# Agent attention and a two-level mixture of experts: first layers of 33 tiles over 128 and 19 rows, and one pool of eight PSUM banks

## Chip, cores and metric

The kernel runs on one core of a Trainium2 chip. The metric is the device time of one execution in microseconds, the median of three runs. One further execution was profiled; all durations and waits below come from it.

## The reference

Four batches of 10048 query rows go through an agent attention and then, each row alone, through the one expert of 16 that a two-level router picks for it. Cut to what matters:

```python
# attention, per batch: 49 agents stand between queries and keys
agent_v = sm(agents, k) @ v                 # 49 x 128
x = sm(q, agents) @ agent_v                 # 10048 x 128

# router: best of 4 groups, then best of 4 experts in it
g_idx = argmax(x @ w_group);  e_idx = argmax(x @ w_expert[g_idx])
h = relu(x @ w1[g_idx, e_idx])              # 128 -> 1024
out = g_weight * e_weight * (h @ w2[g_idx, e_idx])   # 1024 -> 128
```

## The kernel before

**Numbers in two halves.** Matrix products with fp16 operands take a value as a high and a low fp16 half. A row of `x` is 49 exponentials times `agent_v`, so the kernel never forms `x`: it folds `agent_v` into the expert's first layer. For each batch, `weights_of` makes a first-layer weight of 49 rows x 1024 columns, doubled to 98 rows, its high half in `ws[:, 0:F]` and its low half in `ws[:, F:2F]`. `query_turn` turns the 49 exponentials' high and low halves into columns: a tile `et` has 98 rows (high, low) and 512 columns, one for each query row.

**Units and tiles.** Most rows of batches one, two and three are computed as if all went to the batch's most frequent expert (`natural`); 20 tiles of 512 rows a batch. A tile has eight units of 128 hidden columns. `first` does a unit's first layer: two products over 98 rows, `et` with the high weights and `et` with the low weights, summed in one PSUM bank `ph`. ScalarE writes relu as fp16 (`hh`), VectorE what is left of it (`hl`). `second` does the unit's second layer: 12 products of 128 columns into the bank `po`, which sums the whole tile. In `run`, `second` of a unit comes eight units after its `first` (`LAG`). `rows_out` scales the tile and stores it.

**What stands between units.** `lanes` holds the other work, the attention of the next batch (`agents_of`, `queries_of`), its router, its weights and the sorting of the rows of the last batch; after each unit, `advance` issues as much of it as the tile's place asks. Each engine takes its instructions in the order of the program. Batch four has no tiles of its own: its rows are gathered by expert and computed in the last part, between the last seven tiles of batch three (`BESIDE`).

**PSUM.** There are eight banks. `ps2` has two, for `po` (and for some tiles while the first attention runs alone); `psa` has six, for `ph` and for the tiles `at` of all other products.

**Loads and stores** are issued by SyncE in the program's order: a copy that waits holds up those behind it.

Of the kernel before, what the change touches and what calls it, by code (L numbers as in the profile page):

```python
# [81 lines left out]
LAG = 8  # L82
WAIT = 0.011
# [74 lines left out]
def build(ctx, tc, qT, kT, v, agT, wr, w1, w2, cpk, out):  # L158
# [13 lines left out]
    ps2 = ctx.enter_context(tc.tile_pool(name="ps2", bufs=2, space=PSUM))  # L172
    psa = ctx.enter_context(tc.tile_pool(name="psa", bufs=6, space=PSUM))
# [5 lines left out]
    def bank(b=1):  # L179

        if alone[0] and b == 0:
            turns[0] += 1
            k = turns[0] % 8
            if k in (1, 4):
                return ps2.tile([P, TQ, C], F32, name="po").rearrange("p a c -> p (a c)")
        return psa.tile([P, 512], F32, name="at", tag="at")
# [41 lines left out]
    ohd = [dram.tile([P, NE, NTP], F16, name=f"ohd{i}") for i in range(B)]  # L228
    wall = dram.tile([NE, P, 2 * F], I32, name="wall")
# [170 lines left out]
    def front(b, early, order, later):  # L400
# [34 lines left out]
        for x in order:  # L435
# [23 lines left out]
            elif o in "sZ":  # L459
                xh, xl = hold["x", f"h{c}" if o == "s" else "q"]  # L460
                y = c if o == "s" else len(chunks)
                ps = psa.tile([P, TS], F32, name="ph", tag="at") if y % 5 < 3 else ps2.tile([P, TQ, C], F32, name="po").rearrange("p a c -> p (a c)")
# [186 lines left out]
    def query_turn(b, ci, x, early):  # L649
        t0, t1 = chunks[ci]  # L650
        for h0 in range(t0, t1, TQ):
# [4 lines left out]
            et = (mo.tile([2 * NA, TS], F16, name="ett", bufs=4) if b == LB else etp.tile([2 * NA, TS], F16, name="et"))[:, 0:(h1 - h0) * P]  # L656
            if b == 0 and h0 // TQ % 4 == 1 and not early:
                vec.tensor_copy(out=et, in_=ptr[0:2 * NA, 0:(h1 - h0) * P])
            else:
                act.activation(et, ptr[0:2 * NA, 0:(h1 - h0) * P], AF.Copy)  # L660
# [5 lines left out]
    def logits_of(b, ci):  # L666
# [8 lines left out]
        for t in range(t0, t1):  # L675
            o = pl[:, (t - t0) * NL:(t - t0 + 1) * NL]
            for h in range(2):
                pe.matmul(o, st["et", t // TQ][:, t % TQ * P:(t % TQ + 1) * P], st["rh"][:, h], start=(h == 0), stop=(h == 1))
# [215 lines left out]
    def weights_of(b, to=None, low=None):  # L894
# [7 lines left out]
        for h in range(2):  # L902
# [5 lines left out]
            yield  # L908
        wv = ws[:, 2 * F:].rearrange("p (k h c) -> p k h c", k=FB, h=2)
# [32 lines left out]
    def first(x, k):  # L942

        w = x["n"]
        ps = psa.tile([P, TS], F32, name="ph", tag="at")
        et = x["et"]
        r = x["per"]
        for j in range(r):
            f = (k * r + j) * P
            for h in range(2):  # L950
                pe.matmul(ps[:, j * w * P:(j + 1) * w * P], x["wb"][0:2 * NA, h * F + f:h * F + f + P], et, start=(h == 0), stop=(h == 1))
        n = r * w * P
        hh, hl = [mo.tile([P, TS], F16, name=name, bufs=LAG + 2) for name in ("hh", "hl")]
# [4 lines left out]
    def second(x, k, hh, hl):  # L958

        if k == 0:  # L960
            x["po"] = ps2.tile([P, TQ, C], F32, name="po")
# [471 lines left out]
```

## Time and profile before

| | |
|---|---|
| median of three runs | 929.74 us |
| the three runs | 926.89, 929.74, 929.83 us |
| the profiled execution | 927.01 us |
| its span, first to last instruction | 925.2 us |
| TensorE busy | 884.6 us, 96% of the span |
| VectorE busy | 686.1 us, 74% |
| ScalarE busy | 601.1 us, 65% |
| GpSimd busy | 507.8 us, 55% |
| granted TensorE clock, mean | 0.994 of full |

Busy times are sums over the span, whose stages have different limits. Products on TensorE overlap their neighbours, so a product's own duration is longer than the distance to the next one; distances between starts say what a product costs.

### The profile page before, as it was taken

The page shows a single profiled execution, that of the slowest core. Times are in us where ns is not written, and L with a number is a line of the kernel's source. Part 1 is how long each engine was busy: PE and PEld are TensorE (multiplying, and loading weights), DVE is VectorE, ACT ScalarE, POOL GpSimd, SP SyncE. Part 2 cuts the span into 40 slices and gives each one's busy share as a digit, 9 for nine tenths or more (in the row PEclk, how much of TensorE's full clock was granted, in tenths as well). Part 3 has the DMA queues.
Part 4 walks back from the last instruction along what each step waited for, and adds up shares of the span by engine and source line. Part 5 has one row for each costly group of instructions (what it writes and reads, how often), then busy time and mean ns, then how long its engine had stood idle before and what let it go on. Part 6 is the DMA issues. An engine that isn't in the chain of part 4 may idle for free.

```text
span 925.2 us, 30602 instructions
## 1 busy us (share of the span) xinstructions
PE 884.6 (96%) x12815; PEld 703.9 (76%) x12815; DVE 686.1 (74%) x1340; ACT 601.1 (65%) x1094; POOL 507.8 (55%) x799
## 2 busy tenths in 40 slices
PE   7889999999999999999999999999999999998996
PEld 6667877787868878787777788767777777776785
DVE  7799889866798765689674667999766666664663
ACT  5486686787668768867773987565555555554552
POOL 2242475364027447415731863135778888888883
PEclk9999999999999999999999999999999999999998
DMA  9682355640168462017853301262353343433331
GB/s 343 226 287 92 91 162 157 195 149 17 39 225 292 128 200 79 25 39 251 295 172 97 112 21 39 110 218 70 118 185 128 126 145 113 133 121 118 119 100 40
DMA packets 61925, 129.03 MB, mean 139 GB/s; under 512 B 7063, under 2 KB 38889, under 8 KB 58321
## 3 DMA queue, kind: packets, MB, share of 16 engines
q1 hardware_dynamic: 56592, 119.75, 38.7%
q0 software_dynamic: 5184, 7.23, 2.9%
q8 instruction: 102, 1.67, 0.8%
q14 instruction: 47, 0.38, 0.1%
HBM read 93.83 MB, written 33.29 MB: 137 GB/s over the span
## 4 chain that ended last, share of the span: by engine, by line
PE 58%; DVE 18%; POOL 4%; ACT 3%; DMA 2%; issue 2%; SPq 0%; POOLq 0%; DVEq 0%; ACTq 0%
PE po L142 29%; PE ph L142 19%; PE at L142 11%; DVE hl L142 8%; POOL out L1243 1%; DVE oh L142 1%; ACT hh L142 1%; POOL gap L1222 1%; DMA er<-erow,gidx 1%; POOL er L1206 1%; DMA xf<-kT 1%; DVE rx L142 1%; DVE oa L142 1%; DMA w2f<-w 1%; DVE oo L142 0%
## 5 line engine op out<-in xcount | busy, mean ns | idle before, releaser
L142 DVE SCALAR_TENSOR_TENSOR hl<-ph,hh 128x512 f16<-128x512 f32 (+1 forms) x642 | 430.2, 679 | 175.7 <-ACT hh L142 174.9
L142 PEld LDWEIGHTS <-hh 128*128 128x128 f16 x5088 | 415.1, 97 | 146.7 <-issue 1.3
L142 ACT ACTIVATE hh<-ph 128x512 f16<-128x512 f32 (+1 forms) x642 | 373.3, 595 | 184.6 <-PE ph L142 180.7
L142 PE MATMUL po<-wbuf,hh 128*128 128x128 f16 x4640 | 451.6, 219 | 1.1 <-DVE wbuf L142 1.1
L142 PE MATMUL po<-wbuf,hl 128*128 128x128 f16 x2320 | 417.8, 219 | 0.0
L142 PE MATMUL ph<-et,wbuf 98*128 98x512 f16 (+1 forms) x960 | 282.1, 376 | 7.5 <-DVE hl L142 5.9
L261 POOL TENSOR_TENSOR xl<-xf,xh 128x256 f16<-128x256 f32 x280 | 178.5, 671 | 177.6 <-ACT xh L142 175.8
L142 PEld LDWEIGHTS <-hl 128*128 128x128 f16 x2544 | 247.7, 97 | 2.2 <-issue 1.3
L142 ACT ACTIVATE xh<-xf 128x1024 f16<-128x1024 f32 x78 | 81.7, 1047 | 42.8 <-PE at L142 24.4
L142 PEld LDWEIGHTS <-wbuf 98*128 98x128 f16 x1184 | 90.0, 99 | 20.6 <-issue 17.9
L988 POOL TENSOR_TENSOR oo<-oo,cw 128x256 f32<-128x256 f32 (+1 forms) x62 | 42.0, 699 | 101.6 <-ACT oo L142 91.8
L1206 POOL DMA_INDIRECT er<-erow,gidx x81 | 83.2, 1027 | 19.1 <-issue 13.8
L1243 POOL DMA_INDIRECT out<-oo,sidx x81 | 80.8, 998 | 19.1 <-issue 11.7
L142 PE MATMUL ph<-ets,wbuf 98*128 98x512 f16 (+1 forms) x224 | 64.2, 372 | 0.0
L646 POOL TENSOR_TENSOR rows<-ef,rows 128x147 f16<-128x147 f32 (+1 forms) x108 | 42.6, 424 | 39.4 <-ACT rows L142 39.4
L1222 POOL MEMSET gap<- 128x320 f16 x162 | 62.5, 386 | 0.1
L142 PEld LDWEIGHTS <-xh 128*128 128x128 f16 x1264 | 56.1, 97 | 4.9 <-issue 3.4
L142 PEld LDWEIGHTS <-xl 128*128 128x128 f16 x632 | 50.4, 96 | 3.0 <-POOL xl L261 1.9
L142 PE MATMUL at<-agh,xl 128*128 128x49 f16 x545 | 51.0, 185 | 1.4 <-POOL xl L261 1.4
L142 PE MATMUL at<-agh,xh 128*128 128x49 f16 x545 | 51.4, 185 | 1.0 <-DVE hl L142 1.0
L142 PE MATMUL at<-agl,xh 128*128 128x49 f16 x545 | 51.0, 185 | 0.0
L142 PE MATMUL at<-vf,S 128*49 128x129 f32 (+1 forms) x632 | 43.9, 278 | 2.6 <-ACT S L142 2.5
(291 smaller groups left out, 895.2 us busy)
## 6 DMA issues: line engine op xcount, KB each, us to landing
xf<-qT SPq DMA_DIRECT2D x38, 512.0 KB, 3.7
vf<-v SPq DMA_DIRECT2D x36, 516.0 KB, 5.0
xf<-kT SPq DMA_DIRECT2D x35, 512.0 KB, 7.0
out<-oo SPq DMA_DIRECT2D x57, 256.0 KB, 3.7
wbuf<-wall SPq DMA_DIRECT2D x14, 1024.0 KB, 4.8
wsg<-wall SPq DMA_DIRECT2D x7, 1024.0 KB, 5.4
erow<-rows SPq DMA_DIRECT2D x3, 1975.0 KB, 8.9
w2f<-w SPq DMA_DIRECT2D x6, 512.0 KB, 4.8
```

Of the source, the lines that this page charges most:

```text
L142: y = f(*a, **k)
L261: eng.tensor_sub(out=xl[:, y], in0=xf[:, y], in1=xh[:, y])
L646: (vec if whole else pool).tensor_sub(out=rows[:, w, NA:2 * NA], in0=ef[:, y], in1=rows[:, w, 0:NA])
L988: pool.tensor_mul(out=o[:, y], in0=o[:, y], in1=state[b]["cw"][:, t + y.start:t + y.stop].broadcast_to([P, y.stop - y.start, C]))
L1206: ins = pool.indirect_dma_start(out=er[:, q], out_offset=None, in_=erow[b][:, :], in_offset=bass.IndirectOffsetOnAxis(ap=place(b, col + q) ...
L1222: tc.keep_in_program_order(pool.memset(gap, 0.0))
L1243: ins = pool.indirect_dma_start(out=out, out_offset=bass.IndirectOffsetOnAxis(ap=place(x["b"], x["col"] + q)[1], axis=0), in_=o[:, q], in_ ...
```

## The change

For tiles of batch two (20) and batch three (13, up to the last seven), the first layer of a unit is cut differently. The product of the low exponentials with the low weights is left out (a term of the size of both halves' rounding). What stays has 98 + 49 = 147 rows: both halves of the exponentials with the high weights, and the high exponentials with the low weights. 128 of them go into one product: rows 98 to 127 of `et` and of the weights, unused so far, get copies of 30 rows (`DUP`). The other 19 rows (`REST`) of four units are done by four products, each with its 19 rows at another quarter of the 128 partitions (`wrest`, `etr`) and into a bank of its own. So a group of four units takes its four banks at once, then come the two large products of units 0 and 1, then those of units 2 and 3 with second layers between them (`STEPS`). `spread` has SyncE copy the rows of a tile, one copy for the 30 and four for the 19.

The two PSUM pools become one of eight banks; batch one still has two of them for its sums, and from batch two on `po` is drawn like all others.

```diff
+GRP = 4
+DUP = P - 2 * NA
+REST = NA - DUP
+ROW = P // GRP
+PACKED = (1, 2)
+STEPS = [[0, 1], [2], [3], []]
...
-    ps2 = ctx.enter_context(tc.tile_pool(name="ps2", bufs=2, space=PSUM))
-    psa = ctx.enter_context(tc.tile_pool(name="psa", bufs=6, space=PSUM))
+    psa = ctx.enter_context(tc.tile_pool(name="psa", bufs=8, space=PSUM))
+    own = [psa.tile([P, 512], F32, name=f"own{i}", tag="at") for i in range(2)]
...
-                return ps2.tile([P, TQ, C], F32, name="po").rearrange("p a c -> p (a c)")
+                return own[k == 4]
...
+    wrest = [const.tile([P, F // GRP], F16, name=f"wrest{i}") for i in range(2)]
...
-            et = (mo.tile([2 * NA, TS], F16, name="ett", bufs=4) if b == LB else etp.tile([2 * NA, TS], F16, name="et"))[:, 0:(h1 - h0) * P]
+            et = (mo.tile([P, TS], F16, name="ett", tag="ett", bufs=DEPTH) if b == LB else etp.tile([P, TS], F16, name="et"))[:, 0:(h1 - h0) * P]
...
+        if to is None and b in PACKED:
+            lows = ws[:, F:2 * F]
+            sync.dma_start(out=ws[2 * NA:P, 0:F], in_=lows[0:DUP])
+            for i in range(GRP):
+                sync.dma_start(out=wrest[b % 2][i * ROW:i * ROW + REST].rearrange("r (g c) -> r g c", c=P),
+                               in_=lows[DUP:NA].rearrange("r (g i c) -> r g i c", i=GRP, c=P)[:, :, i])
...
-        ps = psa.tile([P, TS], F32, name="ph", tag="at")
...
-        for j in range(r):
-            f = (k * r + j) * P
-            for h in range(2):
-                pe.matmul(ps[:, j * w * P:(j + 1) * w * P], x["wb"][0:2 * NA, h * F + f:h * F + f + P], et, start=(h == 0), stop=(h == 1))
         n = r * w * P
+        if "wr" in x:
+            pe.pin = tc.keep_in_program_order
+            if k % GRP == 0:
+                x["ph"] = [psa.tile([P, TS], F32, name="ph", tag="at") for _ in range(GRP)]
+                for i, ps in enumerate(x["ph"]):
+                    y = slice(i * ROW, i * ROW + REST)
+                    pe.matmul(ps[:, 0:n], x["wr"][y, k // GRP * P:(k // GRP + 1) * P], x["rest"][y, 0:n], start=True, stop=False)
+            ps = x["ph"][k % GRP]
+            pe.matmul(ps[:, 0:n], x["wb"][:, k * P:(k + 1) * P], x["full"], start=False, stop=True)
+            pe.pin = None
+        else:
+            ps = psa.tile([P, TS], F32, name="ph", tag="at")
+            for j in range(r):
+                f = (k * r + j) * P
+                for h in range(2):
+                    pe.matmul(ps[:, j * w * P:(j + 1) * w * P], x["wb"][0:2 * NA, h * F + f:h * F + f + P], et, start=(h == 0), stop=(h == 1))
...
-            x["po"] = ps2.tile([P, TQ, C], F32, name="po")
+            po = own[x["w"] % 2] if x["b"] == 0 and x["done"] is rows_out else psa.tile([P, TS], F32, name="po", tag="at")
+            x["po"] = po.rearrange("p (a c) -> p a c", c=C)
...
-        return dict(b=b, w=w, t=t, n=n, per=1, units=FB, et=state[b]["et", w], apart=b > 0 and (b < LB - 1 or w < NW - BESIDE - 2),
-                    wb=wbuf[b % 2].bitcast(F16), done=rows_out)
+        x = dict(b=b, w=w, t=t, n=n, per=1, units=FB, et=state[b]["et", w][0:2 * NA], apart=b > 0 and (b < LB - 1 or w < NW - BESIDE - 2),
+                 wb=wbuf[b % 2].bitcast(F16), done=rows_out)
+        if packed(b, w):
+            x["full"], x["wr"] = state[b]["et", w], wrest[b % 2]
+        return x
+
+    def packed(b, w):
+
+        return b in PACKED and (b < LB - 1 or w < NW - BESIDE)
+
+    def spread(b, w):
+
+        st = state.get(b, {})
+        if not packed(b, w) or ("et", w) not in st or ("rest", w) in st:
+            return
+        et = st["et", w]
+        st["rest", w] = r = mo.tile([P, TS], F16, name="etr", bufs=2)
+        sync.dma_start(out=et[2 * NA:P], in_=et[0:DUP])
+        for i in range(GRP):
+            sync.dma_start(out=r[i * ROW:i * ROW + REST, 0:et.shape[1]], in_=et[DUP:NA])
...
-        er = mo.tile([P, TQ, RW], I32, name="er", bufs=DEPTH)
+        er = mo.tile([P, TQ, RW], I32, name="er", tag="ett", bufs=DEPTH)
...
+        lag = LAG
+        if "wr" in x:
+            lag = LAG - 1
+            spread(x["b"], x["w"])
+            x["rest"] = state[x["b"]]["rest", x["w"]]
...
-            pending.append(first(x, k))
-            if len(pending) > LAG:
+            for i in STEPS[k % GRP] if "wr" in x else [k % GRP]:
+                pending.append(first(x, k // GRP * GRP + i))
+            while len(pending) > lag + (("wr" in x) and k % GRP < GRP - 1):
                 second(*pending.pop(0))
...
+    ahead = [(b, w) for b in range(LB) for w in range(NW - BESIDE if b == LB - 1 else NW)]
...
             run(natural(b, w), b + w / NW)
+            for y in ahead[ahead.index((b, w)):][1:2]:
+                spread(*y)
```

How the instructions stand. First TensorE at the start of batch two before the change (`wbuf1` are its weights, `wbuf0` those of batch one, whose last units' second layers stand between; `DVE_49` is VectorE's counter, and all lines name the helper that records instructions):

```order
L142 LDWEIGHTS wbuf1_105
L142 MATMUL ph_6251<-et_3902,wbuf1_105 128x512 [waits DVE_49]
L142 LDWEIGHTS wbuf1_105
L142 MATMUL ph_6251<-et_3902,wbuf1_105 128x512
L142 LDWEIGHTS hh_5995
L142 MATMUL po_6258<-wbuf0_104,hh_5995 128x128
...
L142 LDWEIGHTS hl_5996
L142 MATMUL po_6258<-wbuf0_104,hl_5996 128x128
L142 LDWEIGHTS wbuf1_105
L142 MATMUL ph_6275<-et_3902,wbuf1_105 128x512 [waits DVE_49]
```

Each unit has two products into one bank, and a wait for VectorE. The same place after the change (`wrest1` are the weights' 19 rows, `etr` those of the tile, `DMAHW` the counters of copies):

```order
L148 LDWEIGHTS wrest1_115 [waits DMAHW4_49]
L148 MATMUL ph_6239<-etr_6233,wrest1_115 128x512 [waits DVE_49]
L148 LDWEIGHTS wrest1_115 [waits DMAHW0_49,DMAHW5_49]
L148 MATMUL ph_6240<-etr_6233,wrest1_115 128x512 [waits DVE_49]
L148 LDWEIGHTS wrest1_115 [waits DMAHW6_49]
L148 MATMUL ph_6241<-etr_6233,wrest1_115 128x512 [waits DVE_49]
L148 LDWEIGHTS wrest1_115 [waits DMAHW7_49]
L148 MATMUL ph_6242<-etr_6233,wrest1_115 128x512 [waits DVE_49]
L148 LDWEIGHTS wbuf1_104 [waits DMAHW3_49]
L148 MATMUL ph_6239<-et_3887,wbuf1_104 128x512
L148 LDWEIGHTS wbuf1_104
L148 MATMUL ph_6240<-et_3887,wbuf1_104 128x512
```

The four small products of a group now stand together, each with a wait of its own for VectorE, which gives back the bank; then follow the large products of the first two units, which have no such wait.

SyncE a little later, after the change (`etr` of the third tile of batch two; `xf` are loads of the attention):

```order
L247 DMA xf_6776<-kT 128x832 [waits DMAHW6_49,Activation_49,Pool_49]
L1022 DMA etr_6740<-et_4032 19x512 [waits DMAHW7_49,PE_49]
L1022 DMA etr_6740<-et_4032 19x512 [waits DMAHW0_49]
L1022 DMA etr_6740<-et_4032 19x512 [waits DMAHW1_49]
L1022 DMA etr_6740<-et_4032 19x512 [waits DMAHW2_49]
L247 DMA xf_7285<-qT 128x1024 [waits DMAHW3_49,Activation_49,Pool_49]
```

Four copies of 19 rows have come between two loads; the first of them waits for TensorE, that is until a buffer of `etr` (there are two) has been used up by the tile two before.

## Rows read from the trace of the kernel before

**Rows 1.** The profile's first part: busy time of each engine in the span.
```profile
PE 884.6 (96%) x12815; PEld 703.9 (76%) x12815; DVE 686.1 (74%) x1340; ACT 601.1 (65%) x1094; POOL 507.8 (55%) x799
```

**Rows 2.** Table by stretches, all engines: length, busy of each, clock, DMA.
```profile
285.00:400.00 115.00, 114.27 (x1847) 92.62 (x1845) 77.89 (x141) 90.14 (x173) 61.68 (x111) 1.00 0.40 123
400.00:440.00 40.00, 38.61 (x518) 29.62 (x516) 38.16 (x81) 27.10 (x47) 15.46 (x24) 1.00 0.49 167
440.00:570.00 130.00, 127.90 (x2022) 103.67 (x2020) 83.84 (x152) 96.36 (x188) 65.23 (x117) 1.00 0.39 125
570.00:656.00 86.00, 82.58 (x1040) 63.57 (x1039) 83.80 (x182) 49.61 (x85) 32.70 (x33) 1.00 0.33 118
...
510.00:550.00 40.00, 38.85 (x683) 32.46 (x682) 26.21 (x47) 37.52 (x77) 31.71 (x59) 1.00 0.25 72
```

**Rows 3.** The same stretches, TensorE's first-layer products (tile ph) alone.
```profile
285.00:400.00 115.00, 45.00 (x152) 1.00 0.40 123
400.00:440.00 40.00, 18.48 (x62) 1.00 0.49 167
440.00:570.00 130.00, 51.42 (x178) 1.00 0.39 125
570.00:656.00 86.00, 40.51 (x137) 1.00 0.33 118
```

**Rows 4.** Timeline of one unit in batch two: start, length, engine, operation.
```profile
330.47 0.60 PE L142 MATMUL ph<-et,wbuf 98*128 98x512 f16 x2
...
331.16 0.60 ACT L142 ACTIVATE hh<-ph 128x512 f16<-128x512 f32 x1 [0.51 <-PE ph L142]
...
331.57 0.60 PE L142 MATMUL ph<-et,wbuf 98*128 98x512 f16 x2
331.79 0.69 DVE L142 SCALAR_TENSOR_TENSOR hl<-ph,hh 128x512 f16<-128x512 f32 x1 [0.41 <-ACT hh L142]
```

**Rows 5.** Timeline around the attention's value products, to the score products' last.
```profile
332.62 0.22 PE L142 MATMUL po<-wbuf,hl 128*128 128x128 f16 x1
332.77 1.09 PE L142 MATMUL at<-vf,S 128*49 128x129 f32 x16
333.79 0.20 PE L142 MATMUL at<-agh,xh 128*128 128x49 f16 x1
...
334.39 0.18 PE L142 MATMUL at<-agh,xl 128*128 128x49 f16 x1
```

**Rows 6.** Timeline of TensorE: two fp32 products of 512 columns.
```profile
425.68 1.08 PE L142 MATMUL at<-w1f,at 128*128 128x512 f32 x2
```

**Rows 7.** Groups by line and form: busy, mean ns of one.
```profile
L142 PE MATMUL ph<-et,wbuf 98*128 98x512 f16 x912 | 270.5, 379 | 7.5 <-DVE hl L142 5.9 <-DVE mch L142 0.9 <-DVE wsg L142 0.6
...
L142 ACT ACTIVATE xh<-xf 128x1024 f16<-128x1024 f32 x71 | 75.2, 1059 | 39.1 <-PE at L142 22.1 <-DMA xf<-kT 9.8 <-POOL rows L646 4.1
...
L142 PE MATMUL at<-vf,S 128*49 128x129 f32 x624 | 42.5, 277 | 2.6 <-ACT S L142 2.5
```

**Rows 8.** TensorE's waits from 285 to 656: total us, times, longest.
```profile
PE ph L142 <- DVE hl L142: 2.2, 6, 0.7
PE at L142 <- POOL rows L646: 1.8, 2, 1.1
```

**Rows 9.** SyncE's queue: its two largest waits, stores' issue, smallest store's landing.
```profile
SPq L993 <- ACT oo L142: 109.0, 19, 11.7
SPq L240 <- POOL xl L261: 59.2, 26, 2.8
...
L993 SPq DMA_DIRECT2D out<-oo x33: 372/394/852, 285.9 to 648.8; - x33
...
out<-oo SPq DMA_DIRECT2D x3, 32.0 KB, 1.8
```

**Rows 10.** Timeline: batch two's weights on VectorE, and its first product.
```profile
275.55 0.68 DVE L142 TENSOR_TENSOR wbuf<-at,wbuf 128x512 f16<-128x512 f32 x1
...
284.96 0.60 PE L142 MATMUL ph<-et,wbuf 98*128 98x512 f16 x2
```

More of the change, by code (lines that the diff above doesn't have):

```diff
@@ L461, in front @@
                 y = c if o == "s" else len(chunks)
-                ps = psa.tile([P, TS], F32, name="ph", tag="at") if y % 5 < 3 else ps2.tile([P, TQ, C], F32, name="po").rearrange("p a c -> p (a c)")
+                ps = psa.tile([P, TS], F32, name="ph", tag="at") if y % 5 < 3 else own[y % 5 - 3]
                 for t in range(t0, t1):
@@ L655, in query_turn @@
                 pe.transpose(ptr[0:2 * NA, (t - h0) * P:(t - h0 + 1) * P], rows[:, t, 0:2 * NA], ident)
-            et = (mo.tile([2 * NA, TS], F16, name="ett", bufs=4) if b == LB else etp.tile([2 * NA, TS], F16, name="et"))[:, 0:(h1 - h0) * P]
+            et = (mo.tile([P, TS], F16, name="ett", tag="ett", bufs=DEPTH) if b == LB else etp.tile([P, TS], F16, name="et"))[:, 0:(h1 - h0) * P]
             if b == 0 and h0 // TQ % 4 == 1 and not early:
-                vec.tensor_copy(out=et, in_=ptr[0:2 * NA, 0:(h1 - h0) * P])
+                vec.tensor_copy(out=et[0:2 * NA], in_=ptr[0:2 * NA, 0:(h1 - h0) * P])
             else:
-                act.activation(et, ptr[0:2 * NA, 0:(h1 - h0) * P], AF.Copy)
+                act.activation(et[0:2 * NA], ptr[0:2 * NA, 0:(h1 - h0) * P], AF.Copy)
             state[b]["et", h0 // TQ] = et
@@ L677, in logits_of @@
             for h in range(2):
-                pe.matmul(o, st["et", t // TQ][:, t % TQ * P:(t % TQ + 1) * P], st["rh"][:, h], start=(h == 0), stop=(h == 1))
+                pe.matmul(o, st["et", t // TQ][0:2 * NA, t % TQ * P:(t % TQ + 1) * P], st["rh"][:, h], start=(h == 0), stop=(h == 1))
             if t % 4 == 3:
@@ L977, in natural @@
         t, n = TILES[w]
-        return dict(b=b, w=w, t=t, n=n, per=1, units=FB, et=state[b]["et", w], apart=b > 0 and (b < LB - 1 or w < NW - BESIDE - 2),
-                    wb=wbuf[b % 2].bitcast(F16), done=rows_out)
+        x = dict(b=b, w=w, t=t, n=n, per=1, units=FB, et=state[b]["et", w][0:2 * NA], apart=b > 0 and (b < LB - 1 or w < NW - BESIDE - 2),
[14 more added lines that the diff above has]
+            sync.dma_start(out=r[i * ROW:i * ROW + REST, 0:et.shape[1]], in_=et[DUP:NA])
     def rows_out(x):
         po, b, n, t = x["po"], x["b"], x["n"], x["t"]
-        o = mo.tile([P, TQ, C], F32, name="oo", bufs=4)
+        o = mo.tile([P, TQ, C], F32, name="oo", tag="oo", bufs=4)
         if x["apart"]:
@@ L1239, in scatter @@
         n = x["n"]
-        o = mo.tile([P, TQ, C], F32, name="oo", bufs=4)
+        o = mo.tile([P, TQ, C], F32, name="oo", tag="oo", bufs=4)
         vec.tensor_mul(out=o[:, 0:n], in0=x["po"][:, 0:n], in1=x["c"].broadcast_to([P, n, C]))
```

## The prediction

> **What bounds the kernel now.** The profiled execution took 927.01 us, 925.2 of them span. The page's first part comes first: TensorE is busy 96% of the span, VectorE 74% [rows 1]. That share is a mean over stages, so the next view is the table by stretches, cut where the limit changes. The packed products start with batch two: its first first-layer product stands at 284.96 [rows 10], and the 33 tiles make 33 x 8 x 2 = 528 products, which the four stretches of [rows 3] hold up to about 656 us (152 + 62 + 178 + 137 = 529). In those 371 us the reader is to see two kinds of stretch [rows 2]. From 285 to 400 and from 440 to 570, 245 us together, TensorE is busy 114.3 of 115 and 127.9 of 130, VectorE two thirds: TensorE sets the pace. From 400 to 440 and from 570 to 656, VectorE is busy 38.2 of 40 and 83.8 of 86, because routing and the sort of the leftover rows are computed there. TensorE is nearly full too, but VectorE leaves only 1.8 + 2.2 us.
>
> In a TensorE-paced stretch the timeline shows one unit [rows 4]: two first-layer products start at 330.47, the next two at 331.57, so a unit costs 1.10 us. The pair shows 0.60 us and one such product lasts 379 ns [rows 7], so the second starts about 0.22 after the first. Two take 0.43, and the 12 second-layer products between take (1.10 - 0.43) / 12 = 0.056 each. TensorE hardly waits at all in the 371 us: the largest entries are 2.2 us for VectorE and 1.8 for GpSimd [rows 8]. A product removed from a TensorE-paced stretch is therefore time removed, if nothing new waits.
>
> **The change, part by part.** *What it removes and adds on TensorE.* Four units have 8 products of 512 columns, 8 x 0.216 = 1.73 us. After the change they have 4 products over 128 rows, 4 x 0.216 = 0.86, and four over 19 rows, each in another quarter of the array. Call the cost of these four, with the change of array layout before and after, S. A group of four units then saves 0.86 - S. There are 66 groups: 19 in the first stretch, 7.75 in the second, 22.25 in the third, 17 in the last (products of [rows 3] over 8). The second layer is the same.
>
> *S, the unknown.* No row shows four products in four row quarters. The nearest are the attention's value products, 49 columns wide, alternately in the left and the right half of the array [rows 5]. Sixteen fp32 instructions of 129 columns take 1.09 us; less the 277 ns of the last [rows 7] that is 15 starts, 54 ns apart. Two fp32 instructions of 512 columns over the whole array take 1.08 us at 0.62 each [rows 6], so they start about 0.46 apart, 0.9 ns a column: 129 columns should take some 115 ns one after another. Half of that was measured, so two parts of the array did run at once. I take the same for four quarters. How fast can four start? The 24 score products of 49 columns start between 333.79 and 334.39 [rows 5], 26 ns apart with their weight loads. Four small products then take 3 x 0.026 + 0.216 = 0.29.
>
> The layout change has a price, and the same rows have it. The last whole-array product starts at 332.62 and would make room at 332.676; the half-array ones begin at 332.77, 0.094 later. The last of them starts at 332.77 + 1.09 - 0.277 = 333.583, is through at 333.637, and the next whole-array product starts at 333.79, 0.153 later. So S = 0.29 + 0.094 + 0.153 = 0.54, and a group saves 0.32 to 0.33. Bounds: below, four at the price of one and no change of layout, S = 0.22 (saves 0.65); above, one after another and both changes, S = 0.86 + 0.25 = 1.11 (loses 0.25). I take 0.54, since its three parts are rows of this kernel.
>
> A full emptying of the array is the costlier reading of these rows: each change waits for the last product's whole duration, 379 - 216 = 163 ns twice, S = 0.29 + 0.33 = 0.62, a saving of 0.24. 41.25 groups would then save 10 us in place of the 13.5 below. The Trainium skill states such a rule, "Mode switching requires drain" (TensorEngine Tiling (Array Packing), Key Properties), and gives no price; the trace agrees in kind, with its 94 and 153 ns [rows 5].
>
> *Where the saving is on the path.* In the TensorE-paced stretches: 41.25 groups x 0.327 = 13.5 us. In the other two, VectorE's work stays, so at most its idle 4.0 us could go; I take 1. ScalarE limits it in one place: from 510 to 550 it is busy 37.5 of 40 [rows 2], so no more than 2.5 us can go there, and 7.5 groups x 0.327 = 2.5 fits just so.
>
> *What is added in waits.* A group now needs four empty banks at once where a unit needed one; the rows of the order show a wait for VectorE on each of the four small products, and behind it stands all of TensorE's work. A bank is freed along this chain [rows 4]: product (0.38), ScalarE's relu 0.60, VectorE's remainder 0.69, with gaps some 1.8 us from the product's start. Two units now come back to back, which queues the second by 0.6. Eight banks less one for the output sum, less those of the attention, leave five or six for eight, so a group needs the banks of the first two or three units of the group before. By the waits written into the program these lie mostly 3.0 to 4.2 us of TensorE work back (a static count with 0.216 and 0.056 a product); the margin over 1.8 to 2.4 is one or two instructions of another kind, and ScalarE's xh of 1059 ns [rows 7] is one. In about 18 groups the bank comes from a ScalarE copy only 1.1 to 2.5 us back (the output sum, which no longer has its own pair of banks, and attention tiles). Lower bound 0; upper, a third of the groups waiting 0.5, 11 us. I take 4 us, nearer the low end, since TensorE's waits for banks are 2.2 us in all now [rows 8].
>
> *What is hidden.* SyncE issues five more copies a tile, 165 in all, and ten for weights. Issuing an output store takes 394 ns, the smallest one lands in 1.8 us [rows 9]; 165 x 0.394 = 65 us of queue time in 371, while the queue already waits 109 + 59 us for just two releasers. A tile's copies may go once the tile two before has made its last small product, 1.5 tiles x 371 / 33 = 17 us ahead, and the copies into rows 98 to 127 far earlier. If that cover went, each tile would begin with 2.2 us of waiting, 33 x 2.2 = 73 us. The weights of batch two are ready at 275.55 + 0.68, 8.7 us before the first product [rows 10], against some 4 us for five copies in a row. Before batch two and after 656 us the same work stands in the same order, and only the choice of banks differs; I give it nothing. The gathered rows of the last stage now share five buffers with the turned rows of batch four, which are used up before.
>
> Sum: 927.0 - 13.5 - 1 + 4 = 916.5. The profiled time lies at the low end of the three runs (926.89, 929.74, 929.83); half of the 2.7 us between it and their median is added: **918 us**.
>
> **The rivals.**
> *1. The small products run one after another* (slower). Place: the row quarters. For it: no row shows four quarters at once. Against: the 54 ns. From S = 0.86 on there is no gain; at 1.11 the stretches that TensorE paces lose 41.25 x 0.25 = 10 us, the others some 2, the waits for banks shrink to 0 to 1: about 940.
> *2. No price for the layout and no new waits.* S = 0.29 or less: 41.25 x 0.57 = 23.5, less 1.8 that ScalarE can't give between 510 and 550 (7.5 x 0.57 = 4.3 against 2.5), plus 1 in the others: about 906. Against it are the 94 and 153 ns.
> *3. The saving comes back as waits for banks.* At 0.33 us of waiting a group, against a margin of one or two instructions, all is given back: 41.25 x 0.33 = 13.5, 927 to 930. For it: eight banks must hold two groups, output sum and attention; against it: the distances above. The Trainium skill warns of this ("Tiling speeds up TensorE but not PSUM evacuation", TensorEngine Tiling (Array Packing), PSUM Bottleneck); the 2.2 us of [rows 8] do not show it yet.
>
> **How the numbers follow.** My sum 0.57; it has its own range, 911 to 925: S from 0.43 (the four at 0.29, half of the layout's price; saves 17.9) to 0.62 (saves 10), waits from 1 to 8 us. Rival 2 has 0.13, rival 3 0.14, rival 1 0.16. Faster means under 926.9, more than 0.3% below 929.74, about what three runs of this kernel can tell from no change: 0.57 + 0.13 = 0.70; same is rival 3, 0.14; slower rival 1, 0.16. The range is 904 to 930: it takes in rivals 2 and 3 and leaves out the slow one and the extreme of the fast one.
>
> **What would show it.** Between 285 and 656 the four small products' starts: some 26 ns apart means they overlap, 216 means rival 1. The next 128-row product should start 0.4 to 0.5 us after the first small one. A group's 48 second-layer products and four large ones with S should make some 4.1 us. TensorE's waits for VectorE or ScalarE at the small products should be near 4 us in all; 13 or more is rival 3. VectorE should be as busy as before from the routing of batch four to its end, and that stretch about as long. A wait of TensorE for SyncE's copies at the start of tiles, or a clock below full, would make all of this wrong.

## The result and the profile after

The changed kernel takes 933.43 us (median of 7 executions, 932.26 to 935.20), the kernel before 929.65 (925.84 to 930.15) beside it: ratio 1.0053, 95% interval 1.0035 to 1.0072. (Ratios and intervals in this document are estimates from all runs; the quotient of the medians, here 1.0041, differs from them by up to 0.25%.) It is slower by 0.5%, against a forecast of 918 us. Its profiled execution has a span of 930.9 us, 5.7 more than before's.

The first part of the page of the changed kernel, against [rows 1]:

```profile
PE 877.5 (94%) x12815; PEld 694.7 (75%) x12815; DVE 684.7 (74%) x1340; ACT 598.1 (64%) x1094; POOL 507.9 (55%) x799
```

Its table by stretches, with the columns of [rows 2] (last but two: granted clock), and two short windows:

```profile
285.00:400.00 115.00, 113.09 (x1915) 92.26 (x1914) 81.11 (x148) 91.67 (x178) 61.53 (x111) 1.00 0.44 135
400.00:440.00 40.00, 38.26 (x532) 28.95 (x530) 37.12 (x79) 26.24 (x46) 18.39 (x28) 0.96 0.55 190
440.00:570.00 130.00, 122.81 (x1970) 98.68 (x1967) 80.61 (x148) 93.76 (x185) 62.73 (x112) 0.97 0.41 129
570.00:656.00 86.00, 78.95 (x977) 58.91 (x976) 82.16 (x176) 46.81 (x81) 29.14 (x29) 0.94 0.35 121
...
442.00:446.00 4.00, 1.85 (x10) 0.57 (x8) 2.39 (x4) 3.49 (x6) 2.83 (x5) 1.00 0.87 275
446.40:449.60 3.20, 3.20 (x33) 2.92 (x32) 1.41 (x3) 2.91 (x5) 2.25 (x4) 0.50 0.60 216
```

Before, TensorE stood still 0.7 of 115, 2.1 of 130 and 3.4 of 86 us, always at full clock [rows 2]. Now it stands still 1.9, 7.2 and 7.1 us, and the clock is below full in three stretches. The last two rows show how: from 442 to 446 TensorE is busy 1.85 of 4 us, and just behind that its clock is granted at 0.50, that is 1.2 GHz, while it is busy all the time.

Its timeline at five places: start, length, engine, operation, and in brackets the idle time before and who ended it:

```profile
277.15 7.10 SPq L920 DMA_DIRECT2D wrest<-wbuf  x4
...
332.86 0.18 PE L148 MATMUL at<-agh,xl 128*128 128x49 f16 x1
332.97 0.40 PE L148 MATMUL ph<-etr,wrest 19*128 19x512 f16 x4
333.30 0.60 PE L148 MATMUL ph<-et,wbuf 128*128 128x512 f16 x2
333.74 0.28 PE L148 MATMUL po<-wbuf,hh 128*128 128x128 f16 x2
...
430.59 6.57 SPq L920 DMA_DIRECT2D wrest<-wbuf  x4
...
437.89 0.44 SPq L247 DMA_DIRECT2D xf<-kT  x1
438.82 2.53 SPq L1022 DMA_DIRECT2D etr<-et  x4
441.40 1.95 SPq L247 DMA_DIRECT2D xf<-kT  x3
442.04 1.06 ACT L148 ACTIVATE xh<-xf 128x1024 f16<-128x1024 f32 x1 [3.81 <-DMA xf<-kT]
442.58 0.38 PE L148 MATMUL ph<-etr,wrest 19*128 19x512 f16 x1 [0.30 <-DMA etr<-et]
444.36 0.37 PE L148 MATMUL ph<-etr,wrest 19*128 19x512 f16 x1 [1.40 <-DVE hl L148]
444.95 0.37 PE L148 MATMUL ph<-etr,wrest 19*128 19x512 f16 x1 [0.23 <-DVE hl L148]
445.55 0.37 PE L148 MATMUL ph<-etr,wrest 19*128 19x512 f16 x1 [0.23 <-DVE hl L148]
...
464.13 1.06 ACT L148 ACTIVATE xh<-xf 128x1024 f16<-128x1024 f32 x1 [4.52 <-PE ph L148]
```

and before the change, the two ScalarE instructions of 442.04 and 464.13, and TensorE's one wait behind the first:

```profile
445.30 1.06 ACT L142 ACTIVATE xh<-xf 128x1024 f16<-128x1024 f32 x1 [3.66 <-DMA xf<-kT]
447.62 0.59 PE L142 MATMUL ph<-et,wbuf 98*128 98x512 f16 x2 [0.70 <-DVE hl L142]
...
461.67 1.06 ACT L142 ACTIVATE xh<-xf 128x1024 f16<-128x1024 f32 x1 [0.97 <-PE at L142]
```

At 332.97 the change does what it is for: four small products run in 0.40 us, hardly longer than one alone (0.38 at 442.58), and the next large one starts at 333.30. From the last score product, which would make room at 332.89, that is 0.41 us for S with both changes of layout. At 442 the same four are spread over 3 us. ScalarE had waited 3.81 us for a load, relus and remainders were late behind it, and each small product waits for the bank of another remainder hl, 0.6 us apart, with no second layer between them.

That wait of ScalarE is not new: before the change, the same instruction waits 3.66 us for its load. But there TensorE, which needs one bank for a unit, works on (busy all 4 us from 442 to 446) and stops once, for 0.70 us. The wait at 464 is new: 4.52 us where it was 0.97. SyncE issues the load for it at 455.98, before the change at 451.82, although the changed kernel is some 5 us ahead at 441.

Waits of TensorE, SyncE and ScalarE from 285 to 656 us (total, times, longest), against [rows 8, 9] (ScalarE waited for loads of kT 3.7 us before, in one wait):

```profile
PE ph L148 <- DVE hl L148: 10.4, 21, 1.5
...
SPq L1022 <- PE ph L148: 62.8, 23, 7.2
...
ACT xh L148 <- DMA xf<-kT: 5.0, 2, 3.8
```

and SyncE's copies into the row quarters in the same stretch (shortest, median, longest issue in ns):

```profile
L1022 SPq DMA_DIRECT2D etr<-et x124: 561/567/1579, 294.3 to 636.7; - x124
```

TensorE's waits for hl went from 2.2 to 10.4 us. This table counts only the time in which TensorE is empty: of the 0.6 us from one late small product to the next it counts 0.23, and the 0.37 in which the small product runs alone come on top. The queue that used to wait for ScalarE's and GpSimd's buffers now waits 62.8 us for TensorE to give a buffer of the small rows back, and one copy takes it 567 ns.

Two accounts are worked out from the traces. The first: for each pair of neighbouring products on TensorE, the usual distance between their starts (the median of the shorter two thirds, over all traces) is the products' own time, and what goes beyond it is lost. From the first first-layer product after 280 us to the first turned tile of gathered rows (280.4 to 663.1 before), in us:

| kernel | length | own time | lost | of it at small products, over 0.15 each | at half clock |
|---|---|---|---|---|---|
| before | 382.8 | 358.7 | 24.1 | none | 0 |
| changed | 385.3 | 329.4 | 55.8 | 24.2 (37 times) | 20.5 |
| e1 | 381.3 | 328.5 | 52.9 | 23.1 (37) | 17.1 |
| e9 | 376.1 | 347.7 | 28.4 | 2.3 (7) | 3.4 |
| e10 | 384.8 | 329.3 | 55.5 | 25.4 (38) | 17.1 |
| e11 | 383.9 | 331.1 | 52.8 | 22.5 (38) | 17.1 |
| e13 | 389.5 | 358.2 | 31.3 | none | 3.4 |
| e15 | 383.0 | 339.1 | 43.9 | 10.7 (18) | 17.1 |
| e16 | 376.9 | 338.9 | 38.0 | 11.7 (21) | 6.8 |
| e17 | 379.3 | 341.5 | 37.8 | 11.1 (18) | 6.8 |

The products need 29.3 us less, 0.44 for each of 66 groups: more than forecast. 31.7 us more are lost: 24.2 at the small products, and 8.1 in pieces under 0.15 us (23.9 against 15.8), with 20.5 us spent at half clock. In these 20.5 us 9.5 are lost, 6.7 of them in such pieces. (The stretch ends where the gathered rows begin. Between some kernels with the same products that point moves by up to 2.5 us of own time, as between e15 and e17.)

The second account: when does the same second-layer product start, later (+) or earlier than before, in us?

| before's time | 286 | 311 | 400 | 441 | 482 | 570 | 612 | 655 |
|---|---|---|---|---|---|---|---|---|
| changed | +2.1 | -1.5 | -4.7 | -4.9 | +0.6 | -2.5 | +1.6 | +2.7 |
| e7 (the change again) | +2.8 | -0.9 | -4.0 | -4.1 | +2.9 | +0.5 | +4.5 | +5.6 |
| e9 | +2.5 | 0.0 | -2.6 | -3.5 | -5.3 | -6.7 | -7.7 | -6.8 |
| e10 | +2.6 | -1.1 | -4.3 | -3.8 | +1.0 | -2.1 | +2.1 | +2.1 |
| e11 | +5.0 | +1.4 | -1.8 | -1.7 | -1.1 | -3.8 | -0.8 | +1.4 |
| e13 | +0.6 | -1.5 | +0.4 | +1.0 | +1.6 | +3.6 | +5.8 | +6.7 |
| e15 | -0.1 | -2.7 | -5.8 | -2.6 | +1.1 | +0.2 | -0.8 | +0.1 |
| e16 | +2.4 | +0.3 | -2.3 | -3.6 | -5.3 | -7.9 | -4.9 | -5.9 |
| e17 | +2.1 | -0.4 | -3.6 | -3.6 | -2.4 | -3.8 | -4.6 | -3.9 |

The changed kernel gains in two stretches (2.1 to -4.7, and 0.6 to -2.5), loses 5.4 us between 441 and 482, and 5.2 between 570 and 655.

### The profile page after: what moved, and what is told of

It reads as the page before. It is cut to its first block, busy times and chain, and to the rows that moved or that the text cites. A ratio compares the mean times of both kernels' runs of the same rounds, so it can differ in the third digit from the quotient of the medians.

```text
span 930.9 us, 30847 instructions
## 1 busy us (share of the span) xinstructions
PE 877.5 (94%) x12815; PEld 694.7 (75%) x12815; DVE 684.7 (74%) x1340; ACT 598.1 (64%) x1094; POOL 507.9 (55%) x799
## 4 chain that ended last, share of the span: by engine, by line
PE 52%; DVE 19%; POOL 5%; ACT 4%; DMA 3%; issue 3%; SPq 0%; POOLq 0%; ACTq 0%; DVEq 0%
PE po L148 22%; PE ph L148 16%; PE at L148 9%; DVE hl L148 9%; PE own L148 4%; POOL er L1249 2%; ACT hh L148 1%; POOL out L1286 1%; DVE oh L148 1%; DMA er<-erow,gidx 1%; DMA xf<-kT 1%; POOL gap L1265 1%; DMA xf<-qT 1%; DVE oa L148 1%; POOL xl L268 1%
## 5 line engine op out<-in xcount | busy, mean ns | idle before, releaser
L148 DVE SCALAR_TENSOR_TENSOR hl<-ph,hh 128x512 f16<-128x512 f32 (+1 forms) x642 | 425.5, 679 | 177.0 <-ACT hh L148 175.4
L148 ACT ACTIVATE hh<-ph 128x512 f16<-128x512 f32 (+1 forms) x642 | 366.8, 594 | 192.2 <-PE ph L148 186.7
L148 PE MATMUL po<-wbuf,hh 128*128 128x128 f16 x3376 | 331.6, 222 | 0.6 <-DVE mch L148 0.6
L148 PE MATMUL po<-wbuf,hl 128*128 128x128 f16 x1688 | 309.0, 222 | 0.0
L148 PEld LDWEIGHTS <-hl 128*128 128x128 f16 x2544 | 250.8, 99 | 2.2 <-issue 1.3
L148 PE MATMUL ph<-et,wbuf 98*128 98x512 f16 (+3 forms) x696 | 217.9, 380 | 4.4 <-DVE hl L148 3.4
L148 PE MATMUL own<-wbuf,hh 128*128 128x128 f16 x1264 | 123.2, 219 | 1.1 <-DVE wbuf L148 1.1
L148 PE MATMUL own<-wbuf,hl 128*128 128x128 f16 x632 | 113.8, 219 | 0.0
L148 ACT ACTIVATE xh<-xf 128x1024 f16<-128x1024 f32 x78 | 81.6, 1047 | 42.9 <-PE at L148 17.1
L148 PEld LDWEIGHTS <-wbuf 98*128 98x128 f16 (+1 forms) x920 | 71.2, 99 | 39.4 <-issue 37.7
L148 PEld LDWEIGHTS <-xh 128*128 128x128 f16 x1264 | 55.5, 96 | 3.4 <-issue 2.2
```

The source lines that it names most:

```text
L148: y = f(*a, **k)
```

## The experiments

Three theories. **A:** the copies in SyncE's queue hold up the attention's loads behind them, and ScalarE, the banks and TensorE wait in turn. **B:** taking four banks at once makes stops out of small delays. **C:** where VectorE paces, and in the tail, nothing can be gained. The runs were made on several chips whose unchanged kernel took 928 to 962 us, so each ratio is to the kernel before on the chip of that run. Up to 655 us the profiles agree well across chips (e3, whose products stand as before's, is within 1.5 us of it there, and 33 us behind at the end). The changed kernel's own second profile, e7, differs from its first by up to 3.0 us in place and by up to 1.6 within a stretch of the table above; smaller differences between two profiles are no finding.

**e1: no copies for the tiles.**

```diff
-            x["full"], x["wr"] = state[b]["et", w], wrest[b % 2]
+            x["full"], x["wr"] = fixed[0][:, 0:n * P] if fixed else state[b]["et", w], wrest[b % 2]
...
         et = st["et", w]
...
+        if fixed:
+            st["rest", w] = fixed[1]
+            return
...
```

> Left out: the five copies that SyncE issues for each of the 33 packed tiles. Every packed tile reads one fixed set of turned rows, filled once, so its first layers are those of the wrong rows; products, banks and second layers stay as in the change. Theory A (the products save what they should, and the copies in SyncE's queue hold back the loads of the attention behind them, so that ScalarE, then the banks, then TensorE wait, and its clock falls): 914 to 922 us, TensorE's waits for VectorE's hl back from 10 us toward 2 to 4, and the granted clock at 1.0 in nearly all windows between 400 and 660. Theory B (the waits come from taking four banks at once and from the shared banks): 930 to 935 us, with the hl waits still near 10 us. Theory C (what is saved is given back in the stretches that VectorE paces and in the tail that GpSimd paces): 925 to 930 us, ahead by 8 us or more at 480, and no more than 3 at 670.

0.9985 of before (0.9965 to 1.0004). Better than the change, far from A's 914 to 922: 23.1 us are still lost at small products. A alone falls.

**e2: the copies without the packing** (the last lines of `natural` are dropped, so all products are as before).

> The copies are issued as in the change, but the products are those of before (two of 98 rows per unit), with the eight shared banks; nothing reads the copies, so SyncE never waits for TensorE with them. Theory A: slower than before by 6 to 15 us (936 to 945), if the time to issue and the landing of earlier transfers is what holds the loads back; about 930 if it is the wait for the buffer that TensorE reads. Theories B and C: 929 to 932, nothing but the price of the shared banks.

1.0278 (1.0256 to 1.0299), and not a measure of the change. No product reads the copies, so nothing holds them to a pace: SyncE issued those of batch two one tile after another from 182 to 258 us, and TensorE stopped once for 18.4 us. Timeline of SyncE and TensorE:

```profile
243.34 1.25 SPq L1020 DMA_DIRECT2D etr<-et  x2
245.10 1.23 SPq L1020 DMA_DIRECT2D etr<-et  x2
247.31 2.45 SPq L1020 DMA_DIRECT2D etr<-et  x4
...
250.71 1.40 PE L148 MATMUL at<-rh,et 98*128 98x21 f16 x47 [18.41 <-DVE rh L148]
```

It shows only how long such copies can fill the queue; that the stop comes from it is likely and was not tried apart.

**e3: the banks alone** (`PACKED = ()`).

> No tile is packed and nothing is copied; left of the change are the eight shared banks and the five shared buffers for batch four's rows. Theory A: as before within 2 us (928 to 932). Theory B: slower by 3 us or more (932 to 936), with TensorE's waits for hl above 5 us. Theory C: as before.

1.0004 (0.9988 to 1.0019): sharing the eight banks costs nothing by itself.

**e4: the copies through GpSimd** (`pool.dma_start` in place of `sync.dma_start` in `spread`).

> The whole change, but the five copies of a tile go through GpSimd's queue, which moves nothing else until its gathers at 650 us. Theory A: the loads come as before and the saving stays, 916 to 924 us, unless GpSimd's own time for issuing (165 copies; its indirect transfers take 1.0 us each) makes its low halves of the attention late, which would show as waits for xl on TensorE and give 926 to 934. Theory B: 931 to 936. Theory C: 926 to 930.

1.0149 (1.0118 to 1.0181), slower than any of the three theories had it. Issuing costs GpSimd 512 ns a copy in the stretch where it makes the attention's low halves, and in order it waits for the buffers too. Its group of these copies, 285 to 656 us, and TensorE's waits, 285 to 670 us:

```profile
L1022 POOL DMA_DIRECT2D etr<-et x124 | 62.7, 512 | 66.0 <-PE ph L148 66.0
```

```profile
PE ph L148 <- DVE hl L148: 11.7, 25, 1.7
PE at L148 <- POOL rows L653: 6.0, 6, 1.5
```

**e5, e6: a lighter VectorE,** without and with the packing.

```diff
+        m = min(n, 2 * P) if short(x) else n
-        vec.scalar_tensor_tensor(out=hl[:, 0:n], ...
+        vec.scalar_tensor_tensor(out=hl[:, 0:m], ...
...
+                if short(x):
+                    s = slice(q % 2 * P, (q % 2 + 1) * P)
```

> Left out: VectorE makes the low half hl for only the first 256 of a tile's 512 columns in the 33 tiles, and the second layers of the other 256 read those again; no tile is packed, nothing is copied, as in e3. It is the base for e6. VectorE loses 264 x about 0.33 us = 87 us of work. Theory C (VectorE paces 400 to 440 and 570 to 650, and takes back there what the products save): TensorE's lost time there goes down and the time falls by 4 to 9 us, no more, since TensorE is the next bound in the unpacked kernel. Theory A and B: the same 4 to 9.

> e1 (packed, no copies for each tile) with the lighter hl of e5; left out are the copies and half of hl. Read it against e5. Theory C: with VectorE out of the way the products' saving of about 0.45 us for each of 66 groups shows: 16 to 26 us below e5, and TensorE's waits for hl under 3 us. If instead the stops come from four banks at once, from late loads or from the chain at the end of each attention, it stays 0 to 8 us below e5, and the stops stand where they stood in e1.

0.9971 (0.9952 to 0.9989) and 0.9910 (0.9878 to 0.9941): the packing is worth 0.6% with a light VectorE, 0.2% with the usual one (e1 against e3), each give or take 0.3 to 0.4%. VectorE's pace is likely a part of it: e6's profile loses 15.1 us at 22 small products, e1's 23.1 at 37. But C's 16 to 26 us do not come. In e12's trace (e6 with five copies moved, below) TensorE's largest waits are single late events of other chains:

```profile
PE at L148 <- ACT xh L148: 4.0, 1, 4.0
PE ph L148 <- DVE hl L148: 2.6, 3, 1.4
PE ph L148 <- DVE over L148: 2.5, 1, 2.5
PE ph L148 <- DVE wsg L148: 2.2, 2, 2.0
```

**e7: the change once more.** 

> The changed kernel itself, on the chip of the other runs of this call: slower than before by 0.3 to 0.7%, for all theories.

1.0032 (1.0010 to 1.0055).

**e8: 16 chosen tiles.**

```diff
-        return b in PACKED and (b < LB - 1 or w < NW - BESIDE)
+        return b == 1 and (w < 8 or w >= 15) or b == 2 and w < 3
```

> The whole change with its copies in SyncE's queue, but packed are only 16 tiles: 0 to 7 and 15 to 19 of batch two and 0 to 2 of batch three, those that TensorE paced and that the changed kernel ran through ahead of before. Theory C: what these tiles save (about 5 us before 400, about 4 from 480 to 566) is kept: 6 to 10 us faster than before. Theory A: the copies still delay the loads in these stretches, 0 to 4 us faster. Theory B: as before or slower, within 3 us.

0.9944 (0.9923 to 0.9965), 5.3 us faster than before. One stop is left, behind the copies of batch three's weights, at the load for which ScalarE waits 3.66 us before the change too; timeline of SyncE, ScalarE and TensorE:

```profile
431.53 6.58 SPq L920 DMA_DIRECT2D wrest<-wbuf  x4
438.23 0.41 SPq L1036 DMA_DIRECT2D out<-oo  x1
438.74 8.28 SPq L247 DMA_DIRECT2D xf<-kT  x5
...
442.98 1.06 ACT L148 ACTIVATE xh<-xf 128x1024 f16<-128x1024 f32 x1 [6.00 <-DMA xf<-kT]
...
445.30 0.27 PE L148 MATMUL po<-wbuf,hh 128*128 128x128 f16 x2 [2.62 <-DVE hl L148]
```

**e9 to e12: these weight copies later,** in e8 (less its tile 0), in the whole change, in e1 and in e6.

```diff
-        if to is None and b in PACKED:
...
+        if to is None and b == 1:
+            copies(b)
...
             run(natural(b, w), b + w / NW)
+            if (b, w) == (1, 17):
+                copies(2)
```

> e8 without its tile 0 of batch two (15 packed tiles), and the five copies of batch three's weights are issued after tile 17 of batch two, some 60 us later, where the queue is less full; the first packed product that needs them is at about 530. In e8 the four small ones took 6.6 us of SyncE from 431.5, the loads behind them began at 438.7, ScalarE waited 6.0 us for the first, and TensorE stopped 2.8 us and then ran a window at half clock. Theory A in its narrowed form (these weight copies make the stop near 445): the stop goes, 2 to 5 us below e8, 0.988 to 0.992 of before. Theory C alone: as e8, since loads would be late there by the memory's own limit.

> The whole change (33 tiles), one edit: the five copies of batch three's weights after tile 17 of batch two. Narrowed theory A: 3 to 6 us less than the change as it was, 0.997 to 1.001 of before, without the stop and the half clock near 445. Theory C: at most 2 us less, since VectorE takes back what comes in 400 to 440 and after 570.

> e1 (left out: the copies of each tile) with the weight copies after tile 17. If the rest of e1's lost saving is the weight copies: 0.991 to 0.995 of before; if it is VectorE's pace and four banks at once: 0.996 to 0.999, with the smalls' waits for hl after 570 as in e1 (some 14 us from 570 to 650).

> e6 (left out: the copies of each tile, and half of hl) with the weight copies after tile 17. Weight copies and VectorE together as the cause: 0.980 to 0.985 of before, 11 to 16 us below e5's 0.997, TensorE's lost time in 400 to 440 down from 10.5 us to under 5. If there is a third cause (chains of the attention and of the routing that TensorE's work used to cover): 0.986 to 0.990.

In the queue they came 16 us later, at 447.5 in e9, not 60. e9: 0.9907 (0.9883 to 0.9932). Its table shows the place where e8 had its stop at full clock, where the changed kernel had 0.50 (ScalarE still waits 4.33 us at that load):

```profile
446.40:449.60 3.20, 3.20 (x68) 2.72 (x66) 3.18 (x6) 3.20 (x7) 3.20 (x6) 1.00 0.92 348
```

e10: 1.0045 (1.0020 to 1.0069), no gain: with 33 tiles ScalarE still waits 4.10 us at the load of 464. e11: 0.9983 (0.9959 to 1.0008), as e1. e12: 0.9906 (0.9878 to 0.9934), as e6, where 0.980 to 0.985 was expected of the weight copies and VectorE. So moving the weight copies shows a gain only in e9, where little else stops TensorE and where tile 0 was dropped as well. e10 against e11, on one chip, gives the price of the tiles' copies in the whole change: 0.62%, 5.8 us; the two intervals leave 0.3 to 1.0%. In the profiles e10 loses 4.8 us between 441 and 482, e11 0.7.

**e13: the bank pattern alone** (all copies are left out as well).

```diff
                 for i, ps in enumerate(x["ph"]):
...
-                    pe.matmul(ps[:, 0:n], x["wr"][y, ...], x["rest"][y, 0:n], start=True, stop=False)
+                    pe.matmul(ps[:, 0:n], x["wb"][0:2 * NA, (k + i) * P:(k + i + 1) * P], et, start=True, stop=False)
...
-            pe.matmul(ps[:, 0:n], x["wb"][:, k * P:(k + 1) * P], x["full"], start=False, stop=True)
+            pe.matmul(ps[:, 0:n], x["wb"][0:2 * NA, F + k * P:F + (k + 1) * P], et, start=False, stop=True)
...
```

> The bank pattern alone. Nothing is packed or copied: each unit has its two products of 98 rows as before, but in the 33 tiles the first products of four units come together, as the small ones do in the change, so that four banks are taken at once, and the second ones stand where the change has its products of 128 rows. Theory B (taking four banks at once turns a short lateness of VectorE into a stop, with the clock's fall behind it): slower than before by 0.4 to 1.0%, with lost time at these first products of 8 us or more. Theory C (the stops are only VectorE's pace, which more TensorE work would hide): 0.998 to 1.002 of before.

1.0104 (1.0074 to 1.0133), 9.8 us. B is shown, for the group's pattern as a whole: the products are those of before (own time 358.2), nothing is copied, and 7.2 us more are lost by the gathered rows. TensorE's timeline has the same steps of 0.6 us, and its waits for hl in the 371 us are 6.9:

```profile
599.06 0.60 PE L148 MATMUL ph<-et,wbuf 98*128 98x512 f16 x2
600.59 0.38 PE L148 MATMUL ph<-et,wbuf 98*128 98x512 f16 x1 [0.93 <-DVE hl L148]
601.18 0.81 PE L148 MATMUL ph<-et,wbuf 98*128 98x512 f16 x3 [0.22 <-DVE hl L148]
```

```profile
PE ph L148 <- DVE hl L148: 6.9, 14, 1.3
```

What e13 keeps of the change beside the banks is the order of the steps in a group and the shorter lag of the second layers; it does not part these from the banks.

**e14 to e18: which tiles lose, and by what.** e14 is e9 without the tiles' copies, e15 e9 with tiles 8 to 14 of batch two, e16 e9 with tiles 3 to 12 of batch three, e17 e15 without the copies, e18 e9 again.

```diff
-        return b == 1 and (1 <= w < 8 or w >= 15) or b == 2 and w < 3
+        return b == 1 and w >= 1 or b == 2 and w < 3                                 # e15, e17
+        return b == 1 and (1 <= w < 8 or w >= 15) or b == 2 and w < NW - BESIDE      # e16
```

> e9 with the tiles' copies left out (all 15 packed tiles read one fixed set of turned rows; the weight copies stay). Theory A: what the tile copies cost in SyncE's queue shows as a gain, 3 to 6 us below e9, 0.984 to 0.988 of before. If they are hidden where TensorE paces: as e9, 0.988 to 0.993.

> e9 with tiles 8 to 14 of batch two packed as well (22 tiles), where VectorE paces (400 to 440) and where the loads of the next attention fill the transfers (440 to 480). Theory A (copies among those loads): 5 to 9 us above e9, 0.996 to 1.000 of before, e16 as e9. Theory B: 3 to 6 us above e9. Theory C: within 2 us of e9, since VectorE's pace only takes the saving back.

> e9 with tiles 3 to 12 of batch three packed as well (25 tiles), where VectorE paces. Theory A: within 2 us of e9, since few loads run there. Theory B (stops and half clock where VectorE is the pace): 4 to 8 us above e9, 0.995 to 0.999 of before. Theory C: within 2 us of e9.

> e15 (22 packed tiles, 8 to 14 of batch two among them) with the tiles' copies left out, as in e14. If it is the copies among the loads that make the middle tiles lose (theory A): 0.990 to 0.994 of before, near e14. If it is the four banks at once (theory B): 0.999 to 1.002, as e15. Between the two, both have a part, in that proportion.

> e9 once more, on the chip of e17: 0.988 to 0.993 of before, for all theories.

| | ratio | interval |
|---|---|---|
| e9, e18 (15 tiles) | 0.9907, 0.9912 | 0.9883 to 0.9932, 0.9896 to 0.9929 |
| e14 (15, no tile copies) | 0.9930 | 0.9906 to 0.9954 |
| e16 (and the end) | 0.9936 | 0.9911 to 0.9961 |
| e15 (and the middle) | 1.0008 | 0.9989 to 1.0028 |
| e17 (and the middle, no tile copies) | 0.9929 | 0.9914 to 0.9944 |

Where TensorE paces, the copies cost nothing that the runs show (e14 against e9; e14's profile is 2.0 us ahead of e9's at 655, too little to tell). The ten end tiles, paced by VectorE, take back all that their products save: 8.8 us of own time, 9.6 more lost. In e16's profile they cost 2.0 us between 570 and 655, in its runs 0.2 to 0.3%, which the intervals do not part from nothing. The seven middle tiles cost 0.9 to 1.0%, and 0.8% of it goes when the copies go. SyncE, ScalarE and TensorE in e15:

```profile
451.33 3.46 SPq L1027 DMA_DIRECT2D etr<-et  x4
455.48 3.20 SPq L934 DMA_DIRECT2D wrest<-wbuf  x3
458.80 1.54 SPq L247 DMA_DIRECT2D xf<-qT  x1
460.45 0.40 SPq L1041 DMA_DIRECT2D out<-oo  x1
460.90 7.13 SPq L247 DMA_DIRECT2D xf<-qT  x4
...
463.99 1.06 ACT L148 ACTIVATE xh<-xf 128x1024 f16<-128x1024 f32 x1 [6.48 <-DMA xf<-qT]
...
466.08 0.27 PE L148 MATMUL po<-wbuf,hh 128*128 128x128 f16 x2 [2.58 <-DVE mch L148]
```

and the same place in e17, where the load is issued 6.8 us earlier and ScalarE hardly waits:

```profile
452.00 7.83 SPq L247 DMA_DIRECT2D xf<-qT  x3
...
461.85 1.06 ACT L148 ACTIVATE xh<-xf 128x1024 f16<-128x1024 f32 x1 [0.54 <-PE at L148]
```

This is the wait at 464 in the changed kernel. Over all traces it is 4.1 to 6.5 us in the four kernels whose queue on SyncE has copies for the middle tiles there (the changed one, e7, e10, e15), and 0.5 to 1.0 us in the sixteen others. So A holds in the middle stretch, where the next attention's loads fill the queue, and C at the end, where nothing can be gained; the waits at the small products, B, stand in both (10.7 and 11.7 us). e15 ran on another chip than e17 and e18. e9 is faster than the kernel before by 0.9%, measured twice.

## Why the prediction was wrong

**Products and S: right in kind, mis-sized to the safe side.** The four small products overlap. S is 0.41 us, not 0.54, and the 0.62 of a full emptying did not come; a group saves 0.44 to 0.45, not 0.327, in all 29.3 us of TensorE's own time. Two slips are small: half of the layout's price makes S 0.41 to 0.42, where 0.43 is written, and from 510 to 550 there are 7 groups, not 7.5.

**The waits for banks: the step that failed first.** "I take 4 us" became 24.2 us, 37 waits of 0.65, beyond the upper bound of 11. By the stretches of the second account, in us:

| before's time | 280 to 400 | 400 to 441 | 441 to 482 | 482 to 570 | 570 to 655 |
|---|---|---|---|---|---|
| paced by | TensorE | VectorE | TensorE | TensorE | VectorE |
| changed: later (+) or earlier by this stretch | -4.7 | -0.2 | +5.4 | -3.1 | +5.2 |
| lost at small products | 2.4 | 3.6 | 5.9 | 1.9 | 10.4 |
| at half clock | 0 | 3.4 | 6.8 | 0 | 10.2 |
| e11 (no copies for the tiles): later or earlier | -1.8 | +0.1 | +0.7 | -2.7 | +5.2 |

The sum had 13.5 - 4 = 9.5 us of gain in TensorE's three stretches; it became 2.4, with 10.2 us lost at small products. The other 14.0 stand in VectorE's two, where the sum counted on no more than 1 us of gain. The estimate asked how far back each bank's last product lies, and allowed for one or two late instructions. It left out what happens once ScalarE or VectorE is late: before, TensorE waited for one bank and did 1.1 us of work per unit while the next remainder (0.69) was made, so it caught up. Now it needs four banks before it may do anything else, and waits for remainder after remainder. At 442 both kernels meet the same late load, and TensorE loses 0.70 us before and some 2 after. e13 shows the loss with the old products, though not apart from the order in the group and the shorter lag. Rival 3 was this mechanism and came nearest; its price, all of the saving and no more, was too low. Its sign, 13 us or more of waits, did not show in the wait table (10.4), which leaves out part of the loss. The page cited for it (the Trainium skill, TensorEngine Tiling (Array Packing), PSUM Bottleneck) is borne out by the 10.4 us of waits and the 24.2 us lost here.

**The copies: not hidden.** The prediction asked whether a tile's copies come in time, and they nearly do (TensorE waits 0.3 us for etr, its weight loads 3.0). It did not ask what stands behind them in SyncE's queue. A copy takes 567 ns, not 394. The copies cost 0.6 to 0.8% (e10 and e11, e15 and e17), and in the profiles e10 loses 4.1 us more than e11 between 441 and 482, e15 5.7 more than e17 between 400 and 482, where a load behind them comes late at 464; TensorE's own waits for them are the 3.3 us above. The Trainium skill lists small transfers as a thing to merge, mostly overhead under 64 KB (DMA: Bandwidth & Descriptors, Rules for kernel authors); these are of 19 KB, and that one takes SyncE longer to issue than a store of 256 KB (567 against 394 ns) agrees. The weights' copies were allowed 4 us of 8.7: four of the five took 7.1 us to issue from 277.15, TensorE's weight loads wait 1.6 us for them, and batch two starts 2.1 us late.

**The clock.** The text said that a clock below full would make it all wrong. It fell to half for 20.5 us of this stretch, six times, each just behind stops of which the longest were 0.5 to 1.5 us. Of the 8.1 us more that are lost in small pieces most belong to it: 6.7 us of such pieces stand in these 20.5 us, and at before's rate (15.8 in 382.8) it would be 0.8. That is read from the account; no run holds the clock up by itself.

**VectorE's stretches: right in the first, wrong in the second.** A saving of 1 us was allowed. From 400 to 441 the changed kernel gains 0.2 us. From 570 to 655 it loses 5.2 (e7 5.1, e10 4.2, e11 5.2, e1 2.6), and e16, with ten packed tiles there, 2.0. That VectorE's work stays explains why nothing is gained. What is lost beyond that stands at the small products, 10.4 us, with 10.2 us at half clock; e13 loses 3.1 there with the old products.

**The tail** was given nothing. In the profiled executions the changed kernel is 2.7 us behind at 655 and 5.7 at the end; the 3.0 are lost between 820 and 880: one wait more for gathered rows, of 1.75 us at 857, and 6.8 us at half clock where it was 3.4. e9 and e18 lose 4 us there too, e17 none. What makes this wait come or stay away is not settled.

The sum by what was measured, up to the gathered rows: 29.3 us saved, 24.2 lost at small products, 8.1 in small pieces, and -0.6 elsewhere (the remainder to the 31.7 lost more): 2.4 us slower.

## What to carry to other kernels

A wait table that shows an idle-free engine says what it costs to remove work there, not how late its suppliers may be: before an engine is made faster, count how many units its buffers let it catch up, and whether the new order takes several buffers before any other work. Before a wait is put down to a change, look whether the same instruction waited before it. Small copies that are themselves in time can still stop the kernel through the loads queued behind them, so put the copies' issue time beside that queue's load in each stretch. A change that gains in some stretches and loses in others is worth splitting by stretch: the same edit on 15 of 33 tiles is 0.9% faster.

## What the runs showed of the hardware

- Four products of 19 rows in four row quarters, with weight loads, take 0.40 us (332.97) where one takes 0.38 (442.58); with both changes of layout it is 0.41 us from where the product ahead of them makes room (332.89) to the start of the next large one (333.30).
- The granted clock fell to 0.50 behind stops: 1.85 us of work in 4 us from 442 was followed by 0.50 from 446.4 to 449.6, with TensorE busy throughout; in e9, busy 3.06 of the first 4 us, it stayed at 1.00.
- Chips differ in the tail: e3, whose products stand in the same order, has 0.5 us less than before at 655 us and 33.2 more at the end on its chip, with 14.2 us of TensorE's waits there put down to issue alone.
